# Seven block products for eight: an output matmul by Strassen's scheme, with float64 weights taken to float32 in fewer steps

## The chip, the cores and the metric

One core of a Trainium2 chip runs the whole kernel as one program. The metric is the device time of that program in microseconds; the median of three runs is given.

## What is computed

Three networks in a row, cut to what matters here:

```python
x  = attention(q, k, v)              # 8 batches, 8 heads, 576 tokens, 64 wide, block-causal
x  = soft_moe(x, phi, w1, w2)        # 4608 tokens, 8 experts of 4 slots, 512 -> 1024 -> 512
h  = x @ w_in                        # w_in  512 x 2048, float64
r  = np.maximum(h, 0.0)
g  = s * (r * r) + b                 # s, b: one number each
out = (g @ w_out).astype(np.float32) # w_out 2048 x 512, float64; out 4608 x 512
```

The last four lines are the dense network that the change rewrites. The mixture in front of it ends in a product of 32 combine weights per token with 32 slot rows, so `x @ w_in` is computed as combine weights times `slots @ w_in` and its contraction is 32 long.

## The kernel before

**Attention and routing** (to about 420 us) run over 32 pairs of heads. Every operation of a pair has a time in the table `SLOT`; `at` collects them in `plan`, and `run` emits them in order of that time. In this part 12 of the 16 tiles of `w_in` and `w_out` are loaded too, as pairs of 32-bit words.

**Experts** (to about 505 us). 16 keys of `w1` and 16 of `w2`, 1 MB each, stream in. Three places (`wpost`) and some more take them; `advance` issues loads while a place is empty, and `used` gives a place back. The loop over the keys calls `expert1` (PE, L806) or `expert2` (L834), then `used`, then `convert(CMOST)`. Between the two halves `mid` copies `hp` to `hs` on ACT (L820), transposes it on PE and writes `hTz` on ACT (L825).

**Conversions.** `from_f64` (L580 and following) is a generator that turns an eighth of `w_in` or `w_out` from float64 words to float32: two ACT conversions (L595, L596), a DVE shift and a DVE merge of the sign (L598, L599), two DVE operations on the low word (L606, L607), and an add (L724 for `w_in`, L686 for `w_out`). Every odd `w_in` key that is merged frees its tile as a place for expert weights (`split`). For `w_out`, `split_wo` goes on: sums of absolute values (L690), a power of two (L695, L697), the scaled high part in float16 on ACT (L707) and the low part on DVE (L712). `convert(most)` steps every active generator once and starts one more while fewer than `most` are active; `CMOST` is 3. Six calls with 2 stand in front of the expert loop.

**Slots and scale** (505 to 527 us). `slot_rows` copies the expert result (`so`, L874) and transposes it. `slots(i)`, eight generators, makes the rows of `slots @ w_in` (L885, L892, L893) and transposes them (L896); between them `convert` runs on. From extremes comes one scale (L914 to L949), and `part_hi` and `part_lo` (L952, L955) write its float16 high and low parts to `mst`.

**Last stage** (from 527 us). 12 groups of 3 x 128 tokens, 16 slices of 128 features: `stage_h` (PE L976, one matmul of 384 columns; ACT Relu L978), `stage_g` (DVE square L984), `stage_r` (float16 high part on ACT L990, low part on DVE L992), `stage_o` (per 128 tokens three matmuls of 512 columns, L1004 to L1006: high x high, high x low, low x high), and at the end of a group `stage_e` (three evictions, L1012 and L1014, and the stores). `ctrans` transposes a group's combine weights (PE L619, copies on ACT L621 and DVE L622). A list `ops_at` holds a time for each of these; `LAG` (4 slices) is how far `stage_o` runs behind `stage_h`. Two h banks and two sets of three o banks fill PSUM.

What sets the order: inside one `with tc.manual_schedule()` section each engine gets its instructions in the order in which the code emits them. There are several such sections (attention; the expert loop; slots and scale; the last stage). Instructions of neighbouring sections can be mixed. Pools opened with `reuse_waits="tile"` let a new tile wait for the old tiles of its place alone.

Of the kernel before, what the change touches and what calls it, by code (L numbers as in the profile page):

```python
# [27 lines left out]
    "r0": -11.8, "x0": -11.6, "r1": -9.8, "x1": -9.6, "r2": -7.8, "x2": -7.6, "r3": -5.8, "x3": -5.6,  # L28
# [8 lines left out]
RND = {"k": "A", "q": "A"}  # L37
# [5 lines left out]
def fused_kernel(  # L43
# [85 lines left out]
    wpow = const.tile([128, 16], F32, name="wpow")  # L129
    lgs = const.tile([128, NT, 32], F32, name="lgs")  # L130
# [47 lines left out]
    MM = [latep.tile([128, 2, 5], F32, name=f"mm_{i}") for i in range(2)]  # L178
    ME = [latep.tile([128, 2, 5], F32, name=f"me_{i}") for i in range(2)]
# [87 lines left out]
    def rough_max(p, r):  # L267
        ps = st.pop(("rps", p, r))
        mm, me = MM[p % 2], ME[p % 2][64:128]
# [31 lines left out]
    def score(p, c):  # L301
        kt, qt, mr = KT[p % 3], QT[p % 3], MR[p % 2]
        ps = st["ps", p, c] = ps_s.tile([128, 2, 512], F32, tag="s", name="s")
        for sl, c0, c1, o in CH[c]:
            ks, qs = slice(128 * sl, 128 * sl + 128), slice(64 + c0, 64 + c1)
            for n, (a, b) in enumerate([(kt[:, ks], qt[:, qs]), (NEG[:, sl, :], mr[:, qs])]):
                for h in range(2):
                    r = slice(64 * h, 64 * h + 64)
                    PE.matmul(ps[:, h, o:o + c1 - c0], a[r], b[r], start=(n == 0), stop=(n == 1))  # L309

# [27 lines left out]
    def sum_lo(p, part):  # L338
        if part == 0:
            st["sl", p] = ring("sl", [128, 2, 576], F16)  # L340
            lo(POOL, st["sl", p][:, :, 0:128], st["pc", p, 2][:, :, 320:448], st["sh", p][:, :, 0:128])
        else:
            lo(POOL, st["sl", p][:, :, 128:576], st.pop(("S", p)), st["sh", p][:, :, 128:576])
# [65 lines left out]
    def route_t(p):  # L409
# [6 lines left out]
        cp("D", xT, ps)  # L416
# [108 lines left out]
    for p in range(NP):  # L525
# [9 lines left out]
        for r in range(4):  # L535
            A(f"r{r}", rough, r)
            A(f"x{r}", rough_max, r)
        A("m_row", m_row)
# [43 lines left out]
    def from_f64(key, finish):  # L582

        w = wt[key]
        v = w.rearrange("p (n t) -> p n t", t=2)
        l32, h32 = v[:, :, 0].bitcast(U32), v[:, :, 1]
        n = w.shape[1] // 2  # L590
        g = P["cv"].tile([128, n], I32, tag="cvg", name="cvg")
        l = P["cv"].tile([128, n], BF16, tag="cvl", name="cvl")
        e = P["cv"].tile([128, n], BF16, tag="cve", name="cve", bufs=1)
        gf = g.bitcast(F32)
        ACT.activation(out=gf, in_=h32.bitcast(F32), func=AF.Copy, scale=2.0 ** -112)  # L595
# [4 lines left out]
        if key[1] % 2:  # L600
            empty.append(split(home[key], key[1]))
            advance()
        yield

        up = g.bitcast(I16).rearrange("p (n t) -> p n t", t=2)[:, :, 1]
        DVE.tensor_scalar(out=e.bitcast(I16), in0=up, scalar1=-128, scalar2=None, op0=ALU.bitwise_and)  # L606
        DVE.tensor_tensor(out=l, in0=l, in1=e, op=ALU.mult)  # L607
        yield
        for fn in finish:
            fn(gf, l)  # L610
            yield
# [3 lines left out]
    def ctrans(g, pool, tag):  # L615

        ps = pool.tile([128, 512], F32, tag=tag, name=tag).bitcast(F16)
        for i in range(3):
            PE.transpose(ps[0:64, 128 * i:128 * i + 128], P["cs"][:, 3 * g + i, :], idH)  # L619
# [490 lines left out]
```

## Time and profile before

| what | value |
|---|---|
| median of three runs | 946.88 us (946.37 to 947.15) |
| time of the profiled execution | 946.0 us |
| its span, first to last instruction | 944.2 us |
| mean granted TensorE clock | 0.972 |
| PE busy | 866.9 us (92%), 6004 matmuls |
| DVE busy | 603.7 us (64%), 1085 instructions |
| ACT busy | 519.5 us (55%), 929 instructions |
| POOL busy | 268.7 us (28%), 248 instructions |

A share of the span is an average over stages with different limits. PE is matmuls, PEld the loads of their weights. A matmul's row is longer than its share of PE's time, since matmuls are pipelined: the distance between two starts tells what one costs. An arrow `out<-in` names the tiles; "x3" is a count.

### The profile page before, as it was taken

The page shows a single profiled execution, that of the slowest core. Times are in us where ns is not written, and L with a number is a line of the kernel's source. Part 1 is how long each engine was busy: PE and PEld are TensorE (multiplying, and loading weights), DVE is VectorE, ACT ScalarE, POOL GpSimd, SP SyncE. Part 2 cuts the span into 40 slices and gives each one's busy share as a digit, 9 for nine tenths or more (in the row PEclk, how much of TensorE's full clock was granted, in tenths as well). Part 3 has the DMA queues.
Part 4 walks back from the last instruction along what each step waited for, and adds up shares of the span by engine and source line. Part 5 has one row for each costly group of instructions (what it writes and reads, how often), then busy time and mean ns, then how long its engine had stood idle before and what let it go on. Part 6 is the DMA issues. An engine that isn't in the chain of part 4 may idle for free.

```text
span 944.2 us, 15561 instructions
## 1 busy us (share of the span) xinstructions
PE 866.9 (92%) x6004; PEld 448.1 (47%) x6004; DVE 603.7 (64%) x1085; ACT 519.5 (55%) x929; POOL 268.7 (28%) x248
## 2 busy tenths in 40 slices
PE   3999999999999999958588799999999999999998
PEld 1565656665656566631022344444444444444443
DVE  5577666766776667449977675565565565565553
ACT  1565646565555555435467465555555555555553
POOL 5575656665666566611000000000000000000000
PEclk9999999999999999967889799999999999999999
DMA  2433424332434233089993000010000100010001
GB/s 77 164 115 102 154 68 151 127 103 88 134 127 143 71 130 130 18 332 368 397 387 116 1 8 27 34 34 1 34 34 1 35 34 1 34 34 12 24 34 33
DMA packets 40313, 92.45 MB, mean 98 GB/s; under 512 B 4592, under 2 KB 4912, under 8 KB 40240
## 3 DMA queue, kind: packets, MB, share of 16 engines
q1 hardware_dynamic: 40240, 91.47, 27.3%
q8 instruction: 47, 0.77, 0.3%
q14 instruction: 26, 0.21, 0.1%
HBM read 81.86 MB, written 9.44 MB: 97 GB/s over the span
## 4 chain that ended last, share of the span: by engine, by line
PE 44%; DMA 4%; DVE 4%; ACT 1%; issue 1%; SPq 0%; DVEq 0%
PE o L1004 13%; PE o L1005 13%; PE o L1006 13%; PE h L976 3%; DMA w<-in_moe_w_dram 3%; DMA w2h<-in_moe_w_dram 1%; DVE cvg L599 1%; ACT cvl L690 0%; DVE cve L606 0%; DVE cvg L686 0%; DVE cvg L598 0%; PE h L619 0%; DVE cvl L607 0%; DVE wi L724 0%; ACT cvg L595 0%
## 5 line engine op out<-in xcount | busy, mean ns | idle before, releaser
L984 DVE SCALAR_TENSOR_TENSOR g<-r,sk 128x384 f32<-128x384 f32 x192 | 119.3, 621 | 126.0 <-ACT r L978 124.4
L978 ACT ACTIVATE r<-h,fo 128x384 f32<-128x384 f32 x192 | 111.1, 579 | 155.4 <-PE h L976 154.3
L314 ACT ACTIVATE pc<-s 128x896 f32<-128x896 f32 (+1 forms) x128 | 107.4, 839 | 137.7 <-PE s L309 128.2
L253 DVE TENSOR_REDUCE mm<-s 128x2 f32<-128x1024 f32 (+3 forms) x128 | 102.5, 823 | 53.4 <-PE s L264 52.6
L309 PE MATMUL s<-qt,kt 64*128 64x448 f32 (+4 forms) x768 | 133.0, 431 | 3.8 <-ACT pc L314 3.5
L992 DVE SCALAR_TENSOR_TENSOR rl<-g,bk,rh 128x384 f16<-128x384 f32 x192 | 118.5, 617 | 8.9 <-ACT rh L990 7.7
L329 POOL TENSOR_TENSOR S<-S,pc 128x640 f32<-128x640 f32 (+2 forms) x96 | 95.8, 998 | 83.3 <-ACT pc L314 78.1
L354 PE MATMUL pv<-pc,rv 128*64 128x448 f32 (+4 forms) x768 | 115.0, 407 | 4.1 <-ACT ot L360 4.1
L990 ACT ACTIVATE rh<-g,bk 128x384 f16<-128x384 f32 x192 | 116.2, 605 | 0.2 <-DVE g L984 0.2
L742 POOL TENSOR_TENSOR c<-lgs,mc 128x192 f32<-128x192 f32 x6 | 3.7, 621 | 351.7 <-DVE mc L740 351.7
L309 PE MATMUL s<-mr,neg 64*128 64x448 f32 (+4 forms) x384 | 95.6, 490 | 0.0
L1006 PEld LDWEIGHTS <-rl 128*128 128x128 f16 x576 | 56.5, 98 | 68.9 <-DVE rl L992 0.9
L1004 PEld LDWEIGHTS <-rh 128*128 128x128 f16 x576 | 56.5, 98 | 66.6 <-issue 0.3
L1005 PEld LDWEIGHTS <-rh 128*128 128x128 f16 x576 | 56.5, 98 | 58.2 <-issue 0.6
L239 POOL TENSOR_TENSOR sl<-S,sh 128x896 f16<-128x896 f32 x32 | 60.6, 1893 | 47.5 <-ACT sh L336 47.5
L309 PEld LDWEIGHTS s<-qt,kt 64*128 64x128 f32 x768 | 59.7, 187 | 27.5 <-ACT pc L314 9.4
L323 POOL TENSOR_TENSOR S<-pc 128x896 f32<-128x896 f32 x32 | 66.9, 2090 | 18.4 <-ACT pc L314 18.4
L264 PE MATMUL s<-kr,qr 64*128 64x64 f32 (+4 forms) x384 | 52.5, 320 | 18.3 <-DVE mm L253 9.0
L976 PE MATMUL h<-ct,mst 128*128 128x384 f16 x192 | 62.7, 329 | 3.8 <-DVE mst L955 3.8
L354 PEld LDWEIGHTS pv<-pc,rv 128*64 128x64 f32 x768 | 43.8, 136 | 36.3 <-issue 12.9
L1004 PE MATMUL o<-wo_0s,rh 128*128 128x512 f16 x144 | 55.3, 384 | 0.0
L1005 PE MATMUL o<-wo_0s,rh 128*128 128x512 f16 x144 | 55.1, 383 | 0.0
(220 smaller groups left out, 1537.0 us busy)
## 6 DMA issues: line engine op xcount, KB each, us to landing
w<-in_moe_w_dram SPq DMA_DIRECT2D x36, 512.0 KB
w2h<-in_moe_w_dram SPq DMA_DIRECT2D x28, 512.0 KB
kt<-in_k_dram SPq DMA_DIRECT2D x32, 320.0 KB
qt<-in_q_dram SPq DMA_DIRECT2D x32, 320.0 KB
rv<-in_v_dram SPq DMA_DIRECT2D x32, 320.0 KB
wi<-in_moe_w_in_dram SPq DMA_DIRECT2D x8, 1024.0 KB
wo<-in_moe_w_out_dram SPq DMA_DIRECT2D x8, 1024.0 KB
out_dram<-ob SPq DMA_DIRECT2D x32, 256.0 KB
```

What stands on the lines that cost most here:

```text
L253: DVE.tensor_reduce(out=o, in_=i, axis=AX, op=ALU.max)
L309: PE.matmul(ps[:, h, o:o + c1 - c0], a[r], b[r], start=(n == 0), stop=(n == 1))
L314: ACT.activation(out=pc[:, :, 0:w], in_=st.pop(("ps", p, c))[:, :, 0:w], func=AF.Exp, scale=scale)
L329: POOL.tensor_tensor(out=x, in0=x, in1=pc[:, :, o:o + c1 - c0], op=ALU.add)
L354: PE.matmul(st["pv", p][r, x[0], x[1]], rv[:, sl, r], pc[:, h, o:o + c1 - c0], start=head, stop=(sl == 4 or c1 <= 128))
L978: ACT.activation(out=r, in_=hps, func=AF.Relu, scale=fo[:, 0:1])
L984: DVE.scalar_tensor_tensor(out=g0, in0=r, scalar=sk[:, f:f + 1], in1=r, op0=ALU.mult, op1=ALU.mult)
L990: ACT.activation(out=rh, in_=g0, func=AF.Identity, bias=bk[:, f:f + 1])
L992: DVE.scalar_tensor_tensor(out=rl, in0=g0, scalar=bk[:, f:f + 1], in1=rh, op0=ALU.add, op1=ALU.subtract)
L1004: PE.matmul(o, rh[:, 128 * i:128 * i + 128], hl[f][0], start=(f == 0), stop=False)
L1005: PE.matmul(o, rh[:, 128 * i:128 * i + 128], hl[f][1], start=False, stop=False)
L1006: PE.matmul(o, rl[:, 128 * i:128 * i + 128], hl[f][0], start=False, stop=(f == 15))
```

## The change

It does four things.

1. *Output products.* A group is now 2 x 128 tokens (18 groups), and four slices of 128 features go together (index j, 4 per group, so 72 steps (g,j)). Tokens and features of a step are cut in two, and so are the features and the columns of `w_out`: 2 x 2 blocks against 2 x 2 blocks. Seven products of block sums (`PROD`) take the place of eight. Each is three float16 matmuls of 256 columns, accumulated over j in one of 14 half banks of PSUM; groups take the 14 halves in turns. `h` has one bank.
2. *Sums of blocks.* `stage_s` squares r on ACT and makes three differences on DVE; `stage_r` writes high and low parts of all seven left sides in one ACT copy and one DVE subtraction of 1792 elements. For `w_out` the sums are made once (`sums`, `high`, `low`). `stage_e` joins the seven results by eight multiply-adds on DVE and one add on POOL, in six pieces spread over the next group.
3. *Scale and bias.* s and b leave the slices: column sums of `w_out` (on PE, in `csum`) times b give a row that is added at the end; a power of two per row of `w_out`, with its root in `crow`, is multiplied into the slots.
4. *float64 to float32.* ACT converts both words, DVE merges them in two operations: the low word becomes the low three bits. All conversions are called before the slots (`CMOST` 2, two calls per key from `w2` on, then a loop that drains the rest), and the `w_in` tiles are used again for r, G and the high and low parts (`room`).

Two smaller edits: the rough maxima of attention are joined by one reduction (`rough_join`) in place of a two-input maximum (L282), and one of their PSUM ranges moves from column 0 to 448.

The diff, cut to its core ("..." where lines are left out):

```diff
     def from_f64(key, finish):
...
-        ACT.activation(out=l, in_=l32, func=AF.Copy, scale=2.0 ** -52)
+        ACT.activation(out=l, in_=l32, func=AF.Copy, scale=0.936 * 2.0 ** -29)
         yield
-        DVE.tensor_scalar(out=g, in0=g, scalar1=3, scalar2=None, op0=ALU.logical_shift_left)
-        DVE.scalar_tensor_tensor(out=g, in0=h32, scalar=-0x80000000, in1=g, op0=ALU.bitwise_and, op1=ALU.bitwise_or)
...
-        DVE.tensor_scalar(out=e.bitcast(I16), in0=up, scalar1=-128, scalar2=None, op0=ALU.bitwise_and)
-        DVE.tensor_tensor(out=l, in0=l, in1=e, op=ALU.mult)
+        DVE.scalar_tensor_tensor(out=g, in0=g, scalar=3, in1=l, op0=ALU.logical_shift_left, op1=ALU.bitwise_or)
+        to = g if finish else wif[key[1]].bitcast(I32)
+        DVE.scalar_tensor_tensor(out=to, in0=h32, scalar=-0x80000000, in1=g, op0=ALU.bitwise_and, op1=ALU.bitwise_or)
...
     def ctrans(g, pool, tag):
-        for i in range(3):
+        for i in range(2):
...
-        ACT.copy(t[0:64], ps[0:64, 0:384])
-        DVE.tensor_copy(t[64:128], ps[0:64, 0:384])
+        ACT.copy(t[0:64], ps[0:64, 0:256])
+        ACT.copy(t[64:128], ps[0:64, 0:256])
...
     def split_wo(i):
...
+        def column_sums(u, s):
+            for h in range(2):
...
+                PE.matmul(P["csum"][a], weven[:, 2 * i + h:2 * i + h + 1].to_broadcast([128, 32]),
+                          u[:, 512 * h:512 * h + 512], start=(n < 4), stop=(n > 11))
+        def roots(u, s):
...
+            ACT.mul(crow[:, 256 * i:256 * i + 256], ps[:, 0:256], 2.0 ** 69)
+        def sums(u, s):
...
+                DVE.tensor_tensor(out=o, in0=a, in1=b, op=op)
+        parts = ((0, 256, 0, 0), (256, 768, 0, 512), (768, 1792, 1, 0))
...
-        return from_f64(("wo", i), [value, power, power2, high, low])
+        return from_f64(("wo", i), [power, power2, scaled, sums, high, low, column_sums, roots])
...
-    T = dict(pe=1, g=0.447, r=1.648)
-    CMOST = 3
+    T = dict(h=(-0.01, 0.24), ct=0.18, hc=0.2, s=0.25, r=1.3, e=(0.58, 0.68, 1.1, 1.6, 2.1, 2.6))
+    CMOST, CPER = 2, [1] * 16 + [2] * 16
...
             used((kind, i))
+            for _ in range(CPER[done['w1'] + done['w2'] - 1]):
+                convert(CMOST)
+        while todo or active:
             convert(CMOST)
-    LAG = 4
+    LAG = 2.8
+    room = {k: [home["wi", i] for i in x] for k, x in (("r", (5, 7)), ("G", (1, 3, 6)), ("rhl", (0, 2, 4)))}
...
         def slots(i):
...
-            (DVE.tensor_copy if i < 7 else ACT.copy)(mf[:, 256 * i:256 * (i + 1)], ps)
+            DVE.tensor_tensor(out=x, in0=ps, in1=crow[:, 256 * i:256 * (i + 1)], op=ALU.mult)
+            DVE.tensor_reduce(out=ext[:, 0, i:i + 1], in_=x, axis=AX, op=ALU.max)
+            DVE.tensor_reduce(out=ext[:, 1, i:i + 1], in_=x, axis=AX, op=ALU.min)
...
+        ACT.activation(out=bsum, in_=P["csum"], func=AF.Copy, scale=b_sb)
...
+        def stage_h(g, j, n):
...
+                PE.matmul(hps[:, 256 * o:256 * o + 256], mst[:, 128 * f:128 * f + 128], ct[g], start=True, stop=True)
+            ACT.activation(out=r[:, n], in_=hps, func=AF.Relu, scale=2.0 ** -22)
+        def stage_s(g, j):
...
+            ACT.activation(out=G[:, 0:4].rearrange("p b n q -> p n b q"), in_=r.rearrange("p n (b q) -> p n b q", q=128),
+                           func=AF.Square)
+            DVE.tensor_tensor(out=G[:, 4:6], in0=G[:, 1:4:2], in1=G[:, 0:2], op=ALU.subtract)
+            DVE.tensor_tensor(out=G[:, 6], in0=G[:, 3], in1=G[:, 4], op=ALU.subtract)
+            DVE.tensor_tensor(out=G[:, 1], in0=G[:, 6], in1=G[:, 2], op=ALU.subtract)
+        def stage_r(g, j):
...
+            ACT.copy(rh, G)
+            DVE.tensor_tensor(out=rl, in0=G, in1=rh, op=ALU.subtract)
+        PROD = ((0, 0), (2, 1), (3, 6), (1, 2), (4, 3), (6, 5), (5, 4))
+        def stage_o(g, j, n, k):
...
+            PE.matmul(o, rh[:, a, n], bh, start=first, stop=False)
+            PE.matmul(o, rh[:, a, n], bl, start=False, stop=False)
+            PE.matmul(o, rl[:, a, n], bh, start=False, stop=last)
...
+        at(0.2, scales)
         for x in range(512, 2048, 512):
+            at(x / 512 - 0.55, part_hi, x, x + 512)
+            at(x / 512 - 0.54, part_lo, x, x + 512)
...
+        for n, (g, j) in enumerate(seq):
+            if j == 2 and g + 1 < NG:
+                at(n + T["ct"], ctrans, g + 1, ps_h, "h")
+            for x in range(2):
+                at(n + T["h"][x] + (T["hc"] if j == 2 and x else 0), stage_h, g, j, x)
+                for n_, k in enumerate(ENDS if j == 3 and x == 1 else REST):
+                    at(n + min(LAG, 1.6 + n * .35) + (7 * x + n_) / 14, stage_o, g, j, x, k)
+            at(n + T["s"] + (T["hc"] if j == 2 else 0), stage_s, g, j)
+            at(n + T["r"] + (T["hc"] if j == 1 else 0), stage_r, g, j)
+            if j == 3:
+                for x in range(6):
+                    at(n + LAG + T["e"][x], step, outs[g])
```

## Rows read from the trace of the kernel before

**Rows 1.** Stretches: busy us and instructions of each engine, clock, DMA share, GB/s

```profile
100.00:400.00 300.00, 287.74 (x2850) 180.46 (x2848) 199.82 (x374) 170.34 (x298) 189.65 (x151) 1.00 0.33 110
420.00:430.00 10.00, 7.43 (x34) 3.25 (x38) 7.76 (x11) 3.50 (x4) 0.89 (x1) 0.51 0.55 169
440.00:505.00 65.00, 46.79 (x210) 9.05 (x207) 54.81 (x72) 40.34 (x65) 0.00 (x0) 0.89 1.00 380
...
600.00:900.00 300.00, 300.00 (x1437) 138.80 (x1436) 176.40 (x317) 169.07 (x317) 7.34 (x12) 1.00 0.07 24
```

**Rows 2.** The page's chain that ended last, by line

```profile
PE o L1004 13%; PE o L1005 13%; PE o L1006 13%; PE h L976 3%; DMA w<-in_moe_w_dram 3%; DMA w2h<-in_moe_w_dram 1%; DVE cvg L599 1%; ACT cvl L690 0%; DVE cve L606 0%; DVE cvg L686 0%; DVE cvg L598 0%; PE h L619 0%; DVE cvl L607 0%; DVE wi L724 0%; ACT cvg L595 0%
```

**Rows 3.** Timeline of one step: start, duration, engine, line, tiles, shapes

```profile
703.95 0.33 PE L976 MATMUL h<-ct,mst 128*128 128x384 f16 x1
704.12 0.38 PE L1004 MATMUL o<-wo_0s,rh 128*128 128x512 f16 x1
704.12 0.10 PEld L1005 LDWEIGHTS <-rh 128*128 128x128 f16 x1
...
706.06 0.33 PE L976 MATMUL h<-ct,mst 128*128 128x384 f16 x1
```

**Rows 4.** Timeline around the transposes of ct, PE

```profile
710.05 0.38 PE L1006 MATMUL o<-wo_0s,rl 128*128 128x512 f16 x1
710.36 0.35 PE L619 MATMUL h<-idH,cs 128*64 128x128 f16 x3
710.65 0.34 PE L976 MATMUL h<-ct,mst 128*128 128x384 f16 x1
```

**Rows 5.** Groups by shape, 560 to 900 us: busy us, mean ns, idle before

```profile
L990 ACT ACTIVATE rh<-g,bk 128x384 f16<-128x384 f32 x160 | 96.8, 605 | 0.0
L978 ACT ACTIVATE r<-h,fo 128x384 f32<-128x384 f32 x160 | 92.7, 579 | 130.6 <-PE h L976 129.6
...
L1014 ACT ACTIVATE ob<-o,fo 128x512 f32<-128x512 f32 x20 | 13.7, 687 | 6.8 <-PE o L1006 6.1
```

**Rows 6.** Groups by shape, 100 to 400 us

```profile
L336 ACT CAST sh<-S 128x896 f16<-128x896 f32 x25 | 23.2, 929 | 0.0
...
L334 ACT CAST sh<-pc 128x256 f16<-128x256 f32 x25 | 10.2, 407 | 0.8
```

**Rows 7.** Groups by shape, 424 to 530 us

```profile
L690 ACT ACTIVATE cvl<-cvg,eps 128x512 bf16<-128x512 f32 x16 | 11.5, 718 | 5.7 <-DVE cvg L686 5.4
...
L599 DVE SCALAR_TENSOR_TENSOR cvg<-wo,cvg 128x1024 int32<-128x1024 int32 x8 | 9.8, 1225 | 0.3
L686 DVE TENSOR_TENSOR cvg<-cvg,cvl 128x1024 f32<-128x1024 f32 x8 | 9.8, 1220 | 0.0
...
L595 ACT ACTIVATE cvg<-wo 128x1024 f32<-128x1024 f32 x8 | 9.3, 1166 | 6.8 <-DVE wi L724 6.8
...
L893 DVE COPY mf<-n 128x256 f32<-128x256 f32 x7 | 2.9, 420 | 1.7 <-PE n L892 1.7
...
L707 ACT ACTIVATE wo_0s<-cvg,wpow 128x512 f16<-128x512 f32 x4 | 2.7, 714 | 0.0
```

**Rows 8.** Timeline of ACT and DVE around the end of routing and mid

```profile
416.54 1.12 ACT L595 ACTIVATE cvg<-wi 128x1024 f32<-128x1024 f32 x1
...
421.77 0.74 DVE L485 SCALAR_TENSOR_TENSOR acc<-acc,f,s 128x512 f32<-128x512 f32 x1
...
470.88 0.67 ACT L820 ACTIVATE hs<-hp,rs 128x512 f32<-128x512 f32 x1
```

**Rows 9.** Timeline from the end of the experts to the last stage

```profile
505.68 0.59 ACT L874 COPY sos<-so 128x512 f32<-128x512 f32 x1 [1.02 <-PE so L834]
...
527.07 0.82 PE L976 MATMUL h<-ct,mst 128*128 128x384 f16 x2 [2.19 <-DVE mst L955]
...
533.27 0.33 PE L976 MATMUL h<-ct,mst 128*128 128x384 f16 x1
```

**Rows 10.** Timeline, the last eviction

```profile
939.50 0.69 ACT L1014 ACTIVATE ob<-o,fo 128x512 f32<-128x512 f32 x1 [0.61 <-PE o L1006]
```

More of the change, by code (lines that the diff above doesn't have):

```diff
@@ L681, in split_wo @@
     def split_wo(i):
-        def value(u, s):
-            DVE.tensor_tensor(out=u, in0=u, in1=s, op=ALU.add)
+        two = slice(2 * i, 2 * i + 2)
         def power(u, s):
             for h in range(2):
-                ACT.activation(out=s[:, 0:512], in_=u[:, 512 * h:512 * h + 512], func=AF.Abs, bias=eps,
+                ACT.activation(out=s[:, 0:512], in_=u[:, 512 * h:512 * h + 512], func=AF.Abs, bias=eps, scale=2.0 ** -10,
                                accum_out=wsum[:, 2 * i + h:2 * i + h + 1])
@@ new lines, in high @@
+        def high(u, s):
+            t = hl[i] = home["wo", i].tile([128, 2, 1792], F16, tag="w", name=f"wo_{i}s")
+            for a, b, w, o in parts:
+                ACT.copy(t[:, 0, a:b], (u, s)[w][:, o:o + b - a])
+        def low(u, s):
+            t = hl[i]
+            for a, b, w, o in parts:
+                DVE.tensor_tensor(out=t[:, 1, a:b], in0=(u, s)[w][:, o:o + b - a], in1=t[:, 0, a:b], op=ALU.subtract)
+            ready.add(i)
+        return from_f64(("wo", i), [power, power2, scaled, sums, high, low, column_sums, roots])
@@ L939, in fused_kernel @@
-        DVE.tensor_tensor(out=bound, in0=mm, in1=gpow, op=ALU.mult)
-        DVE.tensor_reduce(out=top[:, 1:2], in_=bound, axis=AX, op=ALU.max)
+        bsum = e1.tile([128, 512], F32, tag="a1", name="bsum")
+        ACT.activation(out=bsum, in_=P["csum"], func=AF.Copy, scale=b_sb)
+        bps = pm.tile([128, 512], F32, tag="m", name="m")
+        PE.matmul(bps, part32, bsum, start=True, stop=True)
+        ACT.copy(brow, bps)
+        POOL.tensor_tensor(out=bdif, in0=brow[:, 256:512], in1=brow[:, 0:256], op=ALU.subtract)
@@ L941, in fused_kernel @@
+        DVE.tensor_reduce(out=top, in_=ext[:, 0], axis=AX, op=ALU.max)
+        DVE.tensor_reduce(out=tmin, in_=ext[:, 1], axis=AX, op=ALU.min)
+        DVE.scalar_tensor_tensor(out=top, in0=tmin, scalar=-1.0, in1=top, op0=ALU.mult, op1=ALU.max)
         gp = pm.tile([128, 512], F32, tag="n", name="n")
-        for n in range(2):
-            PE.matmul(gp[:, 128 * n:128 * n + 128], top[:, n:n + 1].to_broadcast([128, 128]), idF, start=True, stop=True)
-        DVE.tensor_reduce(out=top, in_=gp[:, 0:256].rearrange("p (a n) -> p a n", a=2), axis=AX, op=ALU.max)
+        PE.matmul(gp[:, 0:128], top.to_broadcast([128, 128]), idF, start=True, stop=True)
@@ L966, in fused_kernel @@
         part_hi(256, 512)
+        part_lo(256, 512)
     ph3.close()
[L968 to L969 removed]
+    ph4.close()
+    ps_h = ctx.enter_context(tc.tile_pool(name="ps_h", bufs=1, space=PSUM, reuse_waits="tile"))
+    ps_o = ctx.enter_context(tc.tile_pool(name="ps_o", bufs=1, space=PSUM, reuse_waits="tile"))
     with tc.manual_schedule():
+        banks = [ps_o.tile([128, 512], F32, name=f"o{i}") for i in range(7)]
@@ new lines, in stage_o @@
+        def stage_o(g, j, n, k):
+            rh, rl = rr_[g, j]
+            i = 2 * j + n
+            assert i in ready
+            a, b = PROD[k]
+            o = acc_of(g, k)
+            first = i == 0 and k in (1, 3, 5, 0)
+            last = i == 7 and k in (2, 4, 6, 0)
+            bh, bl = (hl[i][:, x, 256 * b:256 * b + 256] for x in range(2))
+            PE.matmul(o, rh[:, a, n], bh, start=first, stop=False)
+            PE.matmul(o, rh[:, a, n], bl, start=False, stop=False)
+            PE.matmul(o, rl[:, a, n], bh, start=False, stop=last)
@@ L1020, in fused_kernel @@
+        ENDS, REST = (0, 5, 6, 1, 2, 3, 4), (1, 2, 3, 4, 5, 6, 0)
+        seq = [(g, j) for g in range(NG) for j in range(4)]
         ops_at = []
```

291 lines of the change are left out of this document (137 added, 154 removed).

## The prediction

> **What bounds the kernel now.** I read the stretches first, then the chain of waits, then single instructions. [Rows 1] are four stretches. From 100 to 400 us (attention) PE is busy 287.74 of 300 us; the change leaves that stretch's PE work alone. From 440 to 505 us the DMA share is 1.00: the expert weights arrive. From 600 to 900 us PE is busy all 300 us at clock 1.00, while DVE has 176.4 us of work and ACT 169.1 us. The chain that ended last [rows 2] lies with 13% on each of L1004, L1005 and L1006, the three products of the output matmul. So the last stage is bound by PE columns, the stretch before it by DMA, and in between a serial chain (slot rows, one scale, first h) has to run. What the Strassen scheme saves counts fully only while PE stays the last to finish.
>
> **The steady last stage.** One step of before, h to h, takes 706.06 - 703.95 = 2.11 us for one matmul of 384 columns and nine of 512 [rows 3]: 4992 columns at 2.4 GHz are 2.08 us, so some 2.5 ns per instruction come on top. 192 steps are 404 us. After, a step (g,j) covers 256 tokens and four slices of 128 features: 4 h matmuls and 2 x 7 x 3 = 42 output matmuls, all of 256 columns. One costs 106.7 + 2.5 = 0.109 us, a step 46 x 0.109 = 5.01 us, and 72 steps 361 us: **43 us less**. Unknown is whether the weight load still hides, since each matmul has its own. At 704.12 the load for L1005 starts with the matmul of L1004 and takes 0.10 us, so it ends before 0.107 us are over: I take 0.109. The bound from above is L619: three transposes of 128 columns in 710.65 - 710.36 = 0.29 us [rows 4], 0.097 each where the columns alone take 0.053; 0.044 more for each of 3312 matmuls would be +145 us. The Trainium skill, page "TensorE: Matmul & The Clock Gate", section "The mechanism", says that a weight load overlaps with running matmuls only when the row group differs; here the row group is the same, and the trace disagrees, since a load of 0.10 us in series would make the step of before 1 us longer than it is. By that sentence every matmul would pay about 0.1 us, over 300 us in all, and the sum would end near 1260 us.
>
> **The transposes of ct.** Before, the pause around them is 710.65 - (710.05 + 0.216) = 0.38 us, 11 times. After there are 17, of two transposes (0.3 us), sharing one h bank. ACT then has two copies of ct where it had one (L622 moves from DVE), which makes it late for the next h; from the walk below I add 0.25. 17 x 0.55 - 11 x 0.38 = **+5 us**.
>
> **ACT and DVE beside it.** ACT per step: two Relu of 512 (at most 0.69 each, L1014 [rows 5]), Square of 1024, copy of 1792 to float16. L336 and L334 (896 in 0.93, 256 in 0.41 us [rows 6]) give 0.82 ns per element and 0.20 fixed: 1.04 and 1.67 us. With h at 0, the first Relu starts at 0.43, the second h follows four triples later, at 1.53, its Relu at 1.95; Square and copy end at about 5.4, just where the next Relu starts (5.01 + 0.43). It may be 0.3 us late before PE's next h waits, so it fits, barely. DVE: subtractions of 512, 256, 256 and 1792, and two of eight fused multiply-adds. L686 (1024 in 1.22) and L893 (256 in 0.42 [rows 7]) give 0.69 + 2 x 0.42 + 2.0 + 2 x 0.48 = 4.5 us. It fits too. L622 and the old evictions L1012 and L1014 are gone from both; they are in these sums by what replaces them.
>
> **The ramp.** Before, the first h starts at 527.07 and the stage runs at full clock from 533.27 [rows 9]; of these 6.2 us some 2.4 are work (three h, nine output products), so 3.8 are lost. After, ACT's order in the hand-written list is Relu, Relu, Square of step 0, scaled part 512, Relu, Relu, Square of step 1, and only then the copy of step 0 (key 1.3 behind 1.25). Counted from the first h: Square(0) ends at 3.6, DVE's differences at 5.1 and part_lo at 5.8, h(1) at 5.9, Square(1) at 9.4, copy(0) at 11.1, the low part at 13.2. Only then can output matmuls flow. The next loops are as serial, because h(2) stands behind six triples of step 0 and copy(1) behind Square(2): low parts ready at about 26.5, 35.8 and 40.3, and PE unbroken from about 40.8. By then it has done three steps of output products and six of h, 16.4 us; 24.4 are lost. **+20.6 us**; bounds are 5 (only the first chain, part of it hidden) and 27 (all of it at the slow pace of the first matmuls of [rows 9], 0.82 us for two h).
>
> **The tail.** Before, one ACT eviction (0.69 us at 939.50 [rows 10]) follows the last matmul; after, four dependent multiply-adds of about 0.45 on DVE. **+1.1 us.**
>
> **The conversions and the start of the stage.** For w_in DVE's four large operations and an add become two of 1.22 us [rows 7]; so split places come free earlier, and part of the lull of 420 to 430 us (169 GB/s against 380 [rows 1], 5.5 us lost) can close: I take 2.5 of 0 to 5. For each eighth of w_out the work grows: ACT two conversions (2.3), two sums of |w| (1.5), two scalings (1.4), three high parts (2.1), one root copy (0.4): 7.7 less overlaps, say 7.4 us; DVE 2 x 1.22, three tiny, 4 x 0.42, and 2.3 for three low parts: 7.0. With CMOST 2 two generators alternate between ACT and DVE; I get 16.2 us per pair. The calls count out as 22 before the expert midpoint, enough for all of w_in and one pair. ACT's queue then stops at hs (470.88 [rows 8], about 468.4 after), as it did before. Three pairs remain: from 476.5 (hTz, first roots and column sums on PE) to 525. All this stands in front of the slot rows in the code; yet sections mix: the third w_in conversion of before (L595 at 416.54 [rows 8]) belongs to the expert loop's section and ran ahead of L485 (421.77) of the section before. So I let slots, with 5 us of ACT and 8 of DVE work, fill the last pair's gaps and stretch it by about 5; the bias row and scale end it, and the first h comes at 532 instead of 527.07: **+5 us**, bounds -3 (all hidden, 2.5 won on the DMA) and +20 (not mixed). SP's queue keeps its order; its loads only get places sooner. PE's added column sums and roots are 1.4 us per eighth beside a DMA-bound stream: nothing, as long as ACT has delivered; PE would wait there otherwise, and the weight places behind it.
>
> **Costed at nothing.** The separate join of the rough maxima (one DVE reduction instead of L282), the shifted PSUM columns and fewer memsets lie under attention's PE, 96% busy; without that cover they are under 1 us per head pair.
>
> **Sum.** 944.2 - 43 + 5 + 20.6 + 1.1 + 5 = 932.9 us span; 1.8 us around it as in the profiled execution (946.0) gives 934.7. The median of the runs, 946.88, is 0.9 above that execution: **935.5 us**, own range 924 to 946.
>
> **Rivals.**
> - *Slots behind the conversions.* If ACT's copy of so keeps its place behind all three pairs, it comes at 525 instead of 505.68 [rows 9]. To the first h it took 21.4 us before, with two conversions in between; without them some 20. First h at 546: 949.5 us, **slower**. For it speaks that the code has one list with a loop that drains all conversions, and ACT's order is fixed in a list; against it the row of 416.54. It comes out slower once the first h starts after 545. Chance 0.20.
> - *ACT is the bound.* If Square and copy together take over 3.15 us, PE waits for the only h bank. L990 (384 in 605 ns [rows 5]) scaled to 1792 is 2.8 us; that would make a step 5.7 us, and half way there is 5.37: 961 us. L336 speaks against it. Chance 0.09.
> - *Ramp mostly absorbed, conversions hidden.* First h at 527 and about 5 us of ramp: 915 us. Before's ramp of 6 us speaks for it, the fixed order of ACT against. Chance 0.15.
> - *Weight loads show* at 256 columns, as in L619: 1080 us. The load rows of [rows 3] speak against it. Chance 0.02.
> - That it saves no columns is excluded by counting: 11,776 x 72 against 4,992 x 192.
>
> **How the numbers follow.** My forecast has 0.54. Range: 918 to 952 us leaves out the ACT and weight cases, the lower half of the absorbed one and the edges: about 0.2. What this measurement can tell from no change is 0.2%, 945 to 948.8. Faster: 0.50 of the forecast, all of the absorbed case, 0.03 of the slots case: 0.68. Same: 0.04 and 0.05: 0.09. Slower: 0.12, 0.09, 0.02: 0.23.
>
> **What would show it.** Output matmuls 0.109 us apart in the middle and about 5.0 us per step (the step); PE holes of 13 and 6 us after the first h, none after 41 us (the ramp); the first h between 528 and 536 us with the copy of so before 515 (the mixing); Square near 1.04 and the copy near 1.67 us (ACT). Wrong it is if PE waits for ACT in every step, if the copy of so comes after 520, or if the ramp has no second hole.

## The result, and the profile after

The changed kernel takes **929.25 us** (median of four runs, 928.23 to 930.74) where the kernel before takes 946.62 in the same comparison: a ratio of 0.982, 95% interval 0.980 to 0.983, so 1.8% faster. The forecast was 935.5, in a range of 918 to 952. The profiled execution after took 930.74 us, the longest of the four, with a span of 928.9, against 944.2 before.

The span is 15.3 us shorter, and two dates split that up. The first h starts at 528.79 instead of 527.07 [rows 9], 1.7 us later; from there to the end it takes 400.1 us instead of 417.1, 17.0 us less.

First the page of the kernel after: busy time and share of each engine, and the chain that ended last.

```profile
PE 841.3 (91%) x7444; PEld 589.5 (63%) x7444; DVE 641.1 (69%) x1121; ACT 595.8 (64%) x858; POOL 311.0 (33%) x266
...
PE 73%; ACT 10%; DVE 7%; DMA 6%; POOL 2%; issue 1%; SPq 0%; POOLq 0%; DVEq 0%; ACTq 0%
PE s L315 12%; PE o L1039 12%; PE o L1041 12%; PE o L1040 12%; PE pv L362 9%; PE tp L247 4%; DMA w<-in_moe_w_dram 4%; PE h L1003 4%; PE s L269 2%; DMA qt<-in_q_dram 2%; ACT pc L322 2%; ACT sh L344 2%; PE tp L386 2%; PE tp L442 1%; DVE mm L255 1%
```

The three products of the output matmul (now L1039 to L1041) hold 12% each instead of 13% [rows 2]: still TensorE's stage. The same stretches as in [rows 1], and ten microseconds from the ramp (columns as there):

```profile
420.00:430.00 10.00, 8.21 (x42) 3.37 (x42) 7.04 (x12) 4.91 (x6) 1.83 (x2) 0.62 0.92 330
440.00:505.00 65.00, 53.17 (x249) 12.19 (x248) 44.98 (x84) 51.90 (x89) 0.00 (x0) 1.00 0.95 359
...
535.00:545.00 10.00, 4.51 (x21) 2.48 (x19) 4.63 (x6) 4.45 (x5) 0.51 (x1) 0.50 0.00 0
...
600.00:900.00 300.00, 300.00 (x2736) 265.48 (x2734) 256.16 (x371) 236.42 (x272) 42.38 (x27) 1.00 0.08 28
```

From 600 to 900 us TensorE is busy all 300 us, as before, but with almost twice as many matmuls; VectorE's work there rose from 176 to 256 us and ScalarE's from 169 to 236. The loads of weights (265.48 us) lie beside these matmuls. The lull of the DMA at 420 to 430 us has closed (330 GB/s for 169). At 535 to 545 the granted clock is 0.50, that is 1.2 GHz. Now one step in the timeline, the answer to [rows 3]; the h matmuls come in pairs, a step runs from 700.56 to 705.58, and PEld is the load of a weight:

```profile
700.56 0.38 PE L1003 MATMUL h<-ct,mst 128*128 128x256 f16 x2
700.78 0.27 PE L1039 MATMUL o<-wo_0s,rhl 128*128 128x256 f16 x1
700.78 0.10 PEld L1040 LDWEIGHTS <-rhl 128*128 128x128 f16 x1
700.89 0.27 PE L1040 MATMUL o<-wo_0s,rhl 128*128 128x256 f16 x1
...
702.09 0.38 PE L1003 MATMUL h<-ct,mst 128*128 128x256 f16 x2
705.58 0.38 PE L1003 MATMUL h<-ct,mst 128*128 128x256 f16 x2
```

The starts are 0.11 us apart and a step takes **5.02 us**, where 0.109 and 5.01 were forecast. The groups by shape of 600 to 900 us tell what ScalarE and VectorE do beside it (busy us, mean ns, idle before):

```profile
L1020 DVE TENSOR_TENSOR rhl<-G,rhl 128x1792 f16<-128x1792 f32 x60 | 121.3, 2022 | 0.0
L1019 ACT CAST rhl<-G 128x1792 f16<-128x1792 f32 x59 | 98.5, 1669 | 0.0
L1004 ACT ACTIVATE r<-h 128x512 f32<-128x512 f32 x118 | 70.3, 596 | 53.0 <-PE h L1003 53.0
L1009 ACT ACTIVATE G<-r 128x1024 f32<-128x1024 f32 x59 | 62.3, 1057 | 1.9
L1011 DVE TENSOR_TENSOR G<-G 128x512 f32<-128x512 f32 x59 | 40.9, 694 | 38.0 <-ACT G L1009 37.5
```

ScalarE waits for h (53.0 us in 59 steps, 0.9 us a step), and hardly ever TensorE for ScalarE. The waits of TensorE from 570 us to the end (us in total, times, longest) are two in all, both for a relu:

```profile
PE h L620 <- ACT r L1004: 1.0, 1, 1.0
PE h L1003 <- ACT r L1004: 0.7, 1, 0.7
```

What the faster stage gives back lies at its start. The timeline of TensorE behind the first h, those rows that begin with an idle time or are an h (start, duration, in brackets the idle time before and what ended it):

```profile
528.79 0.39 PE L1003 MATMUL h<-ct,mst 128*128 128x256 f16 x2 [2.03 <-DVE mst L971]
...
534.53 0.61 PE L1003 MATMUL h<-ct,mst 128*128 128x256 f16 x2 [4.21 <-DVE mst L971]
...
539.77 0.39 PE L1039 MATMUL o<-wo_0s,rhl 128*128 128x256 f16 x1 [3.35 <-ACT rhl L1019]
541.83 0.39 PE L1041 MATMUL o<-wo_0s,rhl 128*128 128x256 f16 x1 [1.45 <-DVE rhl L1020]
545.21 0.64 PE L1003 MATMUL h<-ct,mst 128*128 128x256 f16 x2
...
552.86 0.28 PE L1039 MATMUL o<-wo_2s,rhl 128*128 128x256 f16 x1 [3.16 <-ACT rhl L1019]
555.76 0.39 PE L1041 MATMUL o<-wo_2s,rhl 128*128 128x256 f16 x1 [2.52 <-DVE rhl L1020]
...
564.99 0.28 PE L1041 MATMUL o<-wo_4s,rhl 128*128 128x256 f16 x1 [0.33 <-DVE rhl L1020]
```

The low parts arrive at 541.83, 555.76 and 564.99, which is 13.0, 27.0 and 36.2 us behind the first h (forecast: 13.2, 26.5, 35.8). The first two times the copy on ScalarE (L1019) is late first, then the subtraction on VectorE (L1020); the third time only the subtraction is, by 0.33 us. In these 36.2 us TensorE is idle for 17.1, and for part of the rest its output matmuls start 0.21 us apart, at the lower clock (542.01 to 546.92 and 556.38 to 560.64). Last, the end of the experts, ScalarE's copies of hs and so in its timeline:

```profile
458.94 0.69 ACT L848 ACTIVATE hs<-hp,rs 128x512 f32<-128x512 f32 x1 [4.03 <-PE csum L711]
...
510.08 0.64 ACT L721 ACTIVATE crow<-roots 128x256 f32<-128x256 f32 x2
510.62 0.57 ACT L908 COPY sos<-so 128x512 f32<-128x512 f32 x1
```

hs is copied 12 us sooner than before [rows 8], and so 5 us later [rows 9], directly behind the last root copy of the conversions.

### The profile page after: what moved, and what is told of

Same layout as the page of the kernel before. It is cut to its first block, busy times and chain, and to the rows that moved or that the text cites. A ratio compares the mean times of both kernels' runs of the same rounds, so it can differ in the third digit from the quotient of the medians.

```text
span 928.9 us, 18238 instructions
## 1 busy us (share of the span) xinstructions
PE 841.3 (91%) x7444; PEld 589.5 (63%) x7444; DVE 641.1 (69%) x1121; ACT 595.8 (64%) x858; POOL 311.0 (33%) x266
## 4 chain that ended last, share of the span: by engine, by line
PE 73%; ACT 10%; DVE 7%; DMA 6%; POOL 2%; issue 1%; SPq 0%; POOLq 0%; DVEq 0%; ACTq 0%
PE s L315 12%; PE o L1039 12%; PE o L1041 12%; PE o L1040 12%; PE pv L362 9%; PE tp L247 4%; DMA w<-in_moe_w_dram 4%; PE h L1003 4%; PE s L269 2%; DMA qt<-in_q_dram 2%; ACT pc L322 2%; ACT sh L344 2%; PE tp L386 2%; PE tp L442 1%; DVE mm L255 1%
## 5 line engine op out<-in xcount | busy, mean ns | idle before, releaser
L255 DVE TENSOR_REDUCE mm<-s 64x4 f32<-64x256 f32 (+5 forms) x224 | 139.3, 635 | 70.5 <-PE s L269 68.3
L1020 DVE TENSOR_TENSOR rhl<-G,rhl 128x1792 f16<-128x1792 f32 x72 | 145.6, 2022 | 0.0
L1004 ACT ACTIVATE r<-h 128x512 f32<-128x512 f32 x144 | 85.8, 596 | 78.4 <-PE h L1003 78.4
L1019 ACT CAST rhl<-G 128x1792 f16<-128x1792 f32 x72 | 120.2, 1670 | 0.2 <-DVE G L1013 0.2
L1039 PEld LDWEIGHTS <-rhl 128*128 128x128 f16 x1008 | 99.4, 99 | 20.7 <-ACT rhl L1019 7.3
L1041 PEld LDWEIGHTS <-rhl 128*128 128x128 f16 x1008 | 99.3, 99 | 17.4 <-DVE rhl L1020 5.3
L1040 PEld LDWEIGHTS <-rhl 128*128 128x128 f16 x1008 | 99.5, 99 | 11.9
L1058 POOL TENSOR_TENSOR z<-u,bdif 128x256 f32<-128x256 f32 x18 | 41.8, 2323 | 189.0 <-DVE u L1044 189.0
L1011 DVE TENSOR_TENSOR G<-G 128x512 f32<-128x512 f32 x72 | 50.1, 695 | 67.0 <-ACT G L1009 66.4
L1009 ACT ACTIVATE G<-r 128x1024 f32<-128x1024 f32 x72 | 76.1, 1057 | 2.3
L1003 PE MATMUL h<-ct,mst 128*128 128x256 f16 x288 | 56.2, 278 | 9.0 <-DVE mst L971 6.2
L269 PEld LDWEIGHTS s<-kr,qr 64*128 64x128 f32 x384 | 36.1, 194 | 32.2 <-issue 12.3
```

Source lines behind the costliest of these rows:

```text
L255: DVE.tensor_reduce(out=o, in_=i, axis=AX, op=ALU.max)
L269: PE.matmul(ps[:, h, o:o + k1 - k0], qt[a, 128 * j:128 * j + 128], kt[a, k0:k1], start=(n == 0), stop=(n == len(RG[r]) - 1))
L1003: PE.matmul(hps[:, 256 * o:256 * o + 256], mst[:, 128 * f:128 * f + 128], ct[g], start=True, stop=True)
L1019: ACT.copy(rh, G)
L1020: DVE.tensor_tensor(out=rl, in0=G, in1=rh, op=ALU.subtract)
L1039: PE.matmul(o, rh[:, a, n], bh, start=first, stop=False)
```

## The experiments

My theory from here: TensorE's columns set a step, the saving of 43 us is that of 8 products to 7, and about half of it is lost in the ramp, which is made by the fixed order on ScalarE and VectorE. The kernel before was timed beside each run, so ratios compare across the groups of runs.

**e1, the copies of the first two steps earlier.**

```diff
-            at(n + T["r"] + (T["hc"] if j == 1 else 0), stage_r, g, j)
+            at(n + (0.47 if n < 2 else T["r"] + (T["hc"] if j == 1 else 0)), stage_r, g, j)
```

> Edit: only the turn of ScalarE's copies of the hidden blocks is moved for the first two steps: the copies of step 0 and step 1 stand directly behind that step's Square and no longer behind the relu and Square of the next step. Theory A (the two holes of TensorE behind the first h are there because ScalarE's fixed order makes the low parts of steps 0 and 1 late): the low parts become ready about 9 us and 15 us after the first h instead of 13.0 and 27.0, the hole of 549 to 556 shrinks to a few us, TensorE is unbroken from about 22 us behind the first h with two steps done instead of 36 us; about 12 to 14 us are saved, 915 to 918 us. Theory B (the holes come from something else that is not ready then, the parts of the output weight or the first o tile's place): no change, 928 to 931 us.

Measured: 921.95 us (918.65 to 926.7), ratio 0.973 (0.969 to 0.977): theory A in kind, 7 us instead of 12 to 14 in size. From the first h (527.51) to the end it took 393.1 us, where the changed kernel takes 400.1. TensorE's timeline of e1 shows what was late next:

```profile
536.64 0.40 PE L1041 MATMUL o<-wo_0s,rhl 128*128 128x256 f16 x1 [0.55 <-DVE rhl L1020]
...
547.69 0.59 PE L1003 MATMUL h<-ct,mst 128*128 128x256 f16 x2 [3.78 <-DVE mst L971]
548.07 0.42 PE L1039 MATMUL o<-wo_2s,rhl 128*128 128x256 f16 x1
548.28 0.42 PE L1040 MATMUL o<-wo_2s,rhl 128*128 128x256 f16 x1
...
554.05 0.27 PE L1039 MATMUL o<-wo_3s,rhl 128*128 128x256 f16 x1
554.15 0.27 PE L1040 MATMUL o<-wo_3s,rhl 128*128 128x256 f16 x1
```

The first low part came at 9.1 us as expected. Then the h of step 2 waited for the scaled part of the first input weight (L971), which stands on VectorE behind step 1's adds; and after that hole the output matmuls start 0.21 us apart at the lower clock, for 5 us, and 0.11 apart again at 554.05. Both losses were missing in my expectation.

**e5, the parts of the input weight earlier; e6, both together.** The edit of e5; e6 has it too, and e1's with n < 3.

```diff
-            at(x / 512 - 0.55, part_hi, x, x + 512)
-            at(x / 512 - 0.54, part_lo, x, x + 512)
+            at((0.1, 0.28, 1.28)[x // 512 - 1], part_hi, x, x + 512)
+            at((0.11, 0.29, 1.29)[x // 512 - 1], part_lo, x, x + 512)
```

> Edit: only the turn of the fp16 high and low parts of the first input weight (ScalarE's scaled copies and VectorE's low parts, three chunks of 512 columns) is moved: each is made about one step earlier, the first between the two relus of step 0, the others behind the Squares of steps 0 and 1; the copies of the hidden blocks stay where the change has them. Theory A (two waits in a row make the ramp: the h matmuls wait for these parts behind VectorE's adds, and the low part of the hidden block waits behind the next step's Square): the h of step 1 comes at 1.5 to 2 us behind that of step 0 instead of 5.7, the first output matmul 3 us earlier, and 3 to 6 us are saved, 923 to 927 us. Theory B (the place of the copies alone sets the ramp, the parts are hidden): within 1 us of 929.

> Edit: the parts of the first input weight are made one step earlier, and the copies of the hidden blocks of steps 0 to 2 stand directly behind that step's Square. Theory A (both waits count, and the one by the parts was what was left of the ramp when the copies alone were moved: TensorE stood from 543.9 to 547.7 there for the part made on VectorE behind the adds of step 1): no hole over 2 us behind the first output matmul, 4 to 8 us less than with the copies alone, 914 to 918 us. Theory B (what is left of the ramp is the low granted clock and the chain relu, Square, adds, copy, low part of the first step): 920 to 922 us as with the copies alone.

Measured: e5 926.35 us (924.82 to 927.37), ratio 0.979 (0.977 to 0.980); e6 919.88 us (918.70 to 920.28), ratio 0.972 (0.970 to 0.973). For e5 theory A holds: the h of step 1 starts 2.5 us behind that of step 0 instead of 5.7 (1.5 to 2 expected), the first output matmul 9.1 us behind the first h instead of 11.0 (3 us sooner expected), and the stage is 396.3 us. e6 lies at the edge of its theory B: 2 us under e1 in the median, whose own runs spread over 8 us, so that the two intervals overlap; in the profiled executions it is 1.9 us under e1 from first h to end (391.2). That the second wait counts is shown by e5 alone; beside the first it gave at most some 2 us and not 4 to 8. Against theory A a hole of 3.17 us was left at 548.30, where the h waits for a relu, and soon behind it the output matmuls were 0.21 us apart (549.23 to 552.43).

**e9, the copies of steps 0 and 2 one relu later than in e6.**

```diff
-            at(n + (0.47 if n < 3 else T["r"] + (T["hc"] if j == 1 else 0)), stage_r, g, j)
+            at(n + ((1.1, 0.47, 1.1)[n] if n < 3 else T["r"] + (T["hc"] if j == 1 else 0)), stage_r, g, j)
```

> Edit to the kernel with both ramp moves: the copies of steps 0 and 2 stand one relu later (behind the first relu of the next step, ahead of its second), since ScalarE idles 1.25 and 1.73 us before them there, waiting for VectorE's adds. Theory A (that idle time holds up the next step's second h matmuls, which then come 4.3 and 3.2 us late): the relu fits into it and 1 to 2 us are saved, 917.5 to 919 us. Theory B (TensorE is then held by the low part of the step before in any case): within 0.5 us of 919.9.

Measured: **917.48 us** (916.27 to 921.96), ratio 0.970 (0.967 to 0.973): theory A by the median, though its runs reach from 916 to 922. The stage of the profiled execution is 387.0 us, 4.2 less than e6's, and the two h that theory A named wait 1.45 us each (532.83 and 550.76) where they waited 4.29 and 3.17 in e6. All idle times of TensorE from 534 to 600 us in e9:

```profile
535.17 0.40 PE L1039 MATMUL o<-wo_0s,rhl 128*128 128x256 f16 x1 [1.76 <-ACT rhl L1019]
537.23 0.40 PE L1041 MATMUL o<-wo_0s,rhl 128*128 128x256 f16 x1 [1.45 <-DVE rhl L1020]
550.76 0.38 PE L1003 MATMUL h<-ct,mst 128*128 128x256 f16 x2 [1.45 <-ACT r L1004]
556.55 0.28 PE L1041 MATMUL o<-wo_6s,rhl 128*128 128x256 f16 x1 [0.17 <-DVE rhl L1020]
560.00 0.27 PE L620 MATMUL h<-idH,cs 128*64 128x128 f16 x2 [0.66 <-ACT r L1004]
565.76 0.38 PE L1003 MATMUL h<-ct,mst 128*128 128x256 f16 x2 [0.68 <-ACT r L1004]
```

Behind the first low part (9.2 us after the first h) only 3.0 us are idle, up to the end of the kernel. By moving three turns in the list, 13 of the 24 us of the ramp came back. This version has the lowest median of all here that do the whole work (e4 leaves work out): by its ratio 11 us under the changed kernel, with an interval that overlaps those of e6 and e1.

**e3, one product twice.**

```diff
+            if k == 6:
+                PE.matmul(o, rh[:, a, n], bh, start=False, stop=False)
+                PE.matmul(o, rh[:, a, n], bl, start=False, stop=False)
+                PE.matmul(o, rl[:, a, n], bh, start=False, stop=False)
             PE.matmul(o, rh[:, a, n], bh, start=first, stop=False)
```

> Edit: the three matmuls of the product with k = 6 are issued twice, so that a step has as many matmuls as eight block products need; the product 6 is counted twice in the output. Theory A (the last stage is set by TensorE's columns alone, and the saving of 43 us is the seventh part of them): 72 steps of two row blocks get 72 x 2 x 3 matmuls more at 0.109 us, 47 us more, about 976 us and steps of 5.7 us. Theory B (ScalarE or VectorE set the pace of a step): their work is unchanged, so the step stays near 5.0 us and the time within 10 us of 930.

Measured: 973.78 us in one run, 44.5 more than the changed kernel; theory A. From one first h of a step to the next TensorE takes 5.68 us (703.17 to 708.85), 0.66 more, which is six matmuls of 0.109. From first h to the end it is 446.1 us, 46.0 more than 400.1, against 47 worked out. So an eighth product would have cost what the count of columns says.

**e4, a third of the output matmuls left out.**

```diff
-            PE.matmul(o, rh[:, a, n], bl, start=False, stop=False)
```

> Edit: the matmul of the high part of the hidden block with the low part of the weight is left out of each product, so a third of the output matmuls of the last stage is gone and that correction is missing in the output. Theory A (VectorE, with 4.5 us of work a step, and ScalarE with 4.4 are the next bound close behind TensorE's 5.0): the step falls only to 4.4 to 4.9 us, the time to 893 to 922 us, and TensorE waits in every step for relu or for the low part. Theory B (TensorE alone matters, the margin is ample): the step falls by 14 x 0.109 = 1.53 us to 3.5 us, 72 x 1.53 = 110 us, to about 820 us.

Measured: 880.84 us in one run; theory A. Of 110 us of TensorE's time 45.6 were gained (first h to end 354.5). The stretch of 600 to 850 us, and three of TensorE's h in its timeline:

```profile
600.00:850.00 250.00, 211.79 (x1803) 172.57 (x1804) 238.43 (x350) 218.78 (x257) 44.27 (x26) 1.00 0.08 29
```
```profile
702.03 0.38 PE L1003 MATMUL h<-ct,mst 128*128 128x256 f16 x2 [0.51 <-ACT r L1004]
704.43 0.38 PE L1003 MATMUL h<-ct,mst 128*128 128x256 f16 x2
706.26 0.38 PE L1003 MATMUL h<-ct,mst 128*128 128x256 f16 x2 [0.57 <-ACT r L1004]
```

VectorE is busy 238.43 of 250 us and TensorE only 211.79; 56 copies L1019 fall into the stretch, so a step takes 4.46 us. That is the next bound, VectorE with ScalarE close behind, 0.56 us a step under the changed kernel. TensorE waits for a relu or a low part there, as theory A said, in most steps. In this order of the list, what TensorE could still save beyond 11% of a step would change nothing.

**e7, the new conversion alone in the kernel before.**

```diff
-        ACT.activation(out=l, in_=l32, func=AF.Copy, scale=2.0 ** -52)
+        ACT.activation(out=l, in_=l32, func=AF.Copy, scale=0.936 * 2.0 ** -29)
...
-        DVE.tensor_scalar(out=g, in0=g, scalar1=3, scalar2=None, op0=ALU.logical_shift_left)
...
-        DVE.tensor_tensor(out=l, in0=l, in1=e, op=ALU.mult)
+        DVE.scalar_tensor_tensor(out=g, in0=g, scalar=3, in1=l, op0=ALU.logical_shift_left, op1=ALU.bitwise_or)
...
-        return from_f64(("wo", i), [value, power, power2, high, low])
+        return from_f64(("wo", i), [power, power2, high, low])
```

> The kernel before, with one part of the change alone: the float64 weights are turned into float32 by two ScalarE and two VectorE instructions (the bits below the high word put in as an integer), without the bfloat16 low part, its exponent and the sum. Theory A (a conversion is not on the path, the last stage has its length by TensorE's columns): the last stage keeps its 417 us, the copy of hs and the copy of so come a few us earlier, 941 to 947 us. Theory B (the conversions set the path from the mixture of experts to the first h, where hs was copied 8.6 us behind its matmuls, so the lighter conversion alone brings a good part of the whole gain): the first h comes 8 us or more earlier, 930 to 938 us, and the seven products gave the less.

Measured: 940.49 us (939.88 to 942.21), ratio 0.994 (0.993 to 0.995), between the theories: half a microsecond better than A's range, 2.5 us short of B's. The first h comes at 520.70, 6.4 us sooner (B: 8 or more), so the conversion is on the path to it, against A; from there the stage takes 417.8 us, as before (417.1), as A said. So the difference of the two profiled executions parts into three: the conversion brings 6.4 us ahead of the stage; what else the change does there takes back 8.1 (520.70 to 528.79); the stage gives 17.7 (417.8 to 400.1). What else it does is the scaling, sums and roots of the output weight, but also the new order that calls all conversions before the slots; no run separates these, and none has the new stage without the new conversion.

**e2, conversions closer together from the start.**

```diff
-    CMOST, CPER = 2, [1] * 16 + [2] * 16
+    CMOST, CPER = 2, [2] * 32
```

> Edit: the conversions of the last sixteen rows of the conversion table go at two per slot from the start instead of at one per slot for the first sixteen. Theory A (the start of the last stage hangs on the copy of so, which stood 7 us in ScalarE's queue behind the last conversions after its matmuls had ended): conversions end earlier, the copy of so comes up to 6 us earlier, and so does the first h: 923 to 927 us. Theory B (denser conversions put VectorE's and ScalarE's work in front of the copies of hs, mid and so, as in the kernel before, where hs was copied 8.6 us behind its matmuls): the pairs of the reduction become slower and the first h comes no earlier: 929 to 940 us.

Measured: 929.44 us (927.22 to 929.70), ratio 0.980 (0.977 to 0.982): no change, and each theory is half right. ScalarE's timeline of e2:

```profile
478.16 0.19 ACT L690 ACTIVATION_READ_ACCUMULATOR cvl<-cvg,eps 128x1 f32 x1
478.25 0.67 ACT L848 ACTIVATE hs<-hp,rs 128x512 f32<-128x512 f32 x1
...
511.44 0.59 ACT L908 COPY sos<-so 128x512 f32<-128x512 f32 x1 [4.93 <-PE so L862]
```

The last product of hp in TensorE's timeline, in e2 and in the changed kernel:

```profile
471.53 1.06 PE L834 MATMUL hp<-w,slotT 128*32 128x512 f32 x8
```
```profile
458.25 0.61 PE L834 MATMUL hp<-w,slotT 128*32 128x512 f32 x3
```

The conversions did end sooner, and the copy of so now waits for so itself, no longer for them. But hs comes 19 us later than in the changed kernel. Some 14 of these arise on TensorE, where the products of hp stand behind column sums that wait for ScalarE (5.42 us at 464.36) and end at 472.6 instead of 458.9; the rest in ScalarE's queue, where hs stands behind the conversions. The last so matmul comes 8 us later. What was won in front of one copy was lost in front of the other.

**e8, the high and low parts of the last two weight blocks left out.**

```diff
+            if i > 5:
+                hl[i] = hl[i - 2]
+                return
             t = hl[i] = home["wo", i].tile([128, 2, 1792], F16, tag="w", name=f"wo_{i}s")
...
         def low(u, s):
+            if i > 5:
+                ready.add(i)
+                return
```

> Edit: the high and low parts of the last two output weight blocks are not made; the output matmuls of these two take the parts of blocks 4 and 5 in their place, so a quarter of the output's sum is of other data. ScalarE loses 3.9 us and VectorE 4.5 us of work ahead of the slots. Theory A (the first h hangs on ScalarE's queue of conversions, behind which the copy of so stands 7 us after its last matmul): the copy of so and the first h come 3.5 to 4 us earlier (copy near 506.7, first h near 525 us), the last stage keeps its 400 us, about 925.5 us. Theory B (the slots wait for VectorE or for the so matmuls, or the slots' own chain absorbs it): the first h moves by less than 1.5 us, 928 to 930 us.

Measured: 926.48 us (925.70 to 928.03), ratio 0.979 (0.977 to 0.981), between the two theories. From the start of the copy of hs to the first h it takes 66.8 us (457.66 to 524.46); in the changed kernel and in e5 69.9, in e1, e3, e4, e6 and e9, which leave this part alone too, 68.3 to 68.4. What divides the two groups is the granted clock in the first slot products. The stretch of 510 to 515 us in the changed kernel and in e1 (columns as in [rows 1]; the clock is third from the end):

```profile
510.00:515.00 5.00, 3.63 (x28) 2.13 (x28) 2.62 (x4) 2.89 (x9) 0.00 (x0) 0.80 0.00 0
```
```profile
510.00:515.00 5.00, 3.77 (x40) 2.16 (x38) 3.07 (x5) 3.06 (x9) 0.00 (x0) 1.00 0.00 0
```

From 510 to 520 us e5 stands at 0.78 and 0.87, and e3, e4, e6, e9 and e8 at 1.00. So at equal clock 1.5 us were won of 3.9, which is theory B's bound; the profiled execution of the changed kernel lost another 1.5 to the clock. The copy of so came at 505.20, but its transposes on TensorE stand behind the column sums and roots of the last two blocks and started at 508.42. ScalarE's queue is a cause, and TensorE's stands close behind it. The stage kept its length (399.5 us).

## Why the prediction was right, and where it was not

*The step.* Forecast 5.01 us and 0.109 per matmul, measured 5.02 and 0.11; e3 shows that the columns set it. The weight loads hide: in [rows 3] as in the step above a load of 0.10 us stands beside a matmul of the same row group. The Trainium skill, page "TensorE: Matmul & The Clock Gate", section "The mechanism", has a sentence that lets a load overlap only where the row group differs; the trace disagrees with it, with 265 us of loads inside 300 us of matmuls. The same section also lets a load run ahead when it goes to a background weight buffer, which the prediction left out and which the trace does not contradict.

*The ramp.* This term held best: +20.6 forecast. Low parts at 13.0, 27.0 and 36.2 us instead of 13.2, 26.5 and 35.8, the two holes where they were expected, and behind 565 us only two waits, of 1.0 us at the transposes (573.81) and 0.7. Up to 564.99 TensorE has work for 11.7 us by counts at full clock, so 24.5 were lost (24.4 forecast): 17.1 idle, and 7.4 in which it worked, mostly at the lower clock. The prediction does not say at which clock its walk ran, so how much of the close agreement is luck stays open. e1, e5, e6 and e9 show the cause: reordering alone takes 13 us of it away. The price of one move alone was misjudged, since the h then waits for the parts of the input weight, and since the clock fell behind the hole that this left: e1's output matmuls were 0.21 us apart for 5 us.

*The start of the stage.* Inside its bounds (+1.7, forecast +5, bounds -3 and +20), but wrong in mechanism, and near in size by luck. The step that failed is "slots, with 5 us of ACT and 8 of DVE work, fill the last pair's gaps and stretch it": nothing mixed. The copy of so stands behind every conversion, at 510.62, while its last matmul had ended at 503.4. That is the first rival's mechanism, and it was priced at 949.5 us because I put the end of the conversions at 525. It came at 510.7: hs was copied at 458.94 and not at 468.4, and a pair took 15.2 us (root copies at 479.57, 494.79, 510.08) instead of 16.2. Before, hs had stood in ScalarE's queue for 8.6 us behind its last product, which ended at 462.3; the prediction kept that wait, and after the change it was gone (458.9 and 458.94). So two errors cancelled: not mixing cost 5 us at the copy of so, and conversions that ended 14 us sooner than priced kept it from costing more. The sign that I had named for mixing, the copy of so before 515, came true without it. What held is the part won on the DMA: the last so matmul ended 2.3 us sooner than before (2.5 forecast). And 1.5 of the +1.7 us are the lower clock in the profiled execution (e8). The row of 416.54 [rows 8], which spoke for mixing, spoke of another pair of sections only. e7 and e8 confirm parts of this: conversions move the first h, and ScalarE's queue is one of the two through which they do.

*ScalarE and VectorE beside it.* Square 1.06 us, copy 1.67, relu 0.60, subtraction 2.02: all within 0.1 us of their terms. The rival that ScalarE is the bound is excluded, but e4 shows how near VectorE's forecast 4.5 us a step are.

*The transposes of ct.* Forecast 0.55 us each, with 0.25 for a late relu. The late relu hardly appears (two waits, 1.7 us in all, behind 570 us); ScalarE has 0.9 us of idle time in a step. What the other terms leave of the stage (400.1 - 417.1 + 43 - 20.7 - 1.7) is 3.6 us instead of 5. *The tail:* from the last matmul's start to the end 6.8 us instead of 5.1, +1.7 for +1.1.

Against the forecast sum of 932.9 the span is 928.9: 3.3 of these 4.0 us are the start of the stage. The median lies some 2 us further below its forecast than the span, since the execution profiled before was 0.9 us under its median and the one after 1.5 above it.

## What to carry to other kernels

When a faster inner step comes with a longer chain from its first input to its first product, count the chain of the first steps by the fixed order of each engine: here it ate half of the gain, and moving three entries of the list brought 13 of 24 us back without touching the work. Work moved ahead of a serial section can be paid for at each copy and product that stands behind it in a queue: e2 moved it and only exchanged one wait for another. And before more is saved on the engine that bounds, take a third of its work away for a trial (e4): it tells how far the next bound is.

## What the hardware showed unexpectedly

GpSimd's add of 128x256 (L1058) takes 2.38 to 2.45 us in the stage and 0.73 at the very end. The timelines of VectorE and GpSimd in the changed kernel, at one of the long ones and at the last:

```profile
885.58 2.02 DVE L1020 TENSOR_TENSOR rhl<-G,rhl 128x1792 f16<-128x1792 f32 x1
```
```profile
885.81 2.38 POOL L1058 TENSOR_TENSOR z<-u,bdif 128x256 f32<-128x256 f32 x1 [18.04 <-DVE u L1044]
...
921.76 0.73 POOL L1058 TENSOR_TENSOR z<-u,bdif 128x256 f32<-128x256 f32 x1 [13.49 <-DVE u L1044]
```

All 17 long ones start within 0.3 us behind the start of VectorE's subtraction of two SBUF tiles and end some 0.6 us behind its end; the short one runs beside a multiply-add that reads PSUM. The Trainium skill, page "GPSIMD Engine Reference", section "1. Specifications", says that GpSimd's SBUF interfaces are shared with VectorE, with contention by VectorE instructions that have two SBUF inputs; these rows agree, though no run moved the add. In the stage it costs nothing here, but an add that someone waits for should not be put there.

The maximum of two 128x10 tiles (L282) took 169 to 1992 ns before, 1128 in the median; the one-input reduction that replaced it (L255) takes 173 to 175 ns each of 32 times. The timelines of VectorE and GpSimd before, at one of the long ones, show the same thing the other way round:

```profile
36.74 1.13 DVE L282 TENSOR_TENSOR mx<-mm,me 128x10 fp32r<-128x10 f32 x1
```
```profile
35.95 1.89 POOL L239 TENSOR_TENSOR sl<-S,sh 128x896 f16<-128x896 f32 x1 [1.40 <-ACT sh L336]
```

It ends with GpSimd's subtraction (37.87 and 37.84). So do all 27 long ones, within 0.1 us of the end of a GpSimd instruction that had begun before them; the five that took 0.17 us began while GpSimd was idle. Attention is bound by TensorE, so this is not seen in the time: its last transposes start at 409.10 us before and at 409.50 after.
